# Long convolution and two MLPs: when the weights are decoded, how the last rows of z come back, when weights are loaded

## The chip, the cores and the metric

The kernel runs on one core of one Trainium2 chip. The metric is the device time of one execution in microseconds. Five engines work from queues of their own: PE (TensorE, the matmuls), DVE (VectorE), ACT (ScalarE), POOL (GpSimd) and SP (SyncE, which issues most DMAs). Each queue is taken in order: an instruction that waits for a semaphore holds up all that stand behind it on its engine.

## The reference, cut to what matters

```python
# x, v: (1, 12480, 128); pos_emb: (12480, 64)
h_filt = (np.maximum(pos_emb @ w1, 0.0) @ w2) * np.exp(-0.01 * pos)[:, None]
y = irfft(rfft(x * v, n=2*S) * rfft(h_filt, n=2*S))[:S]     # causal convolution, per channel
x = x * y
h = x @ moe_w_in;  g = np.where(h > 0, h, np.exp(np.minimum(h, 0)) - 1);  x = g @ moe_w_out
h = x @ moe2_w_in; g = np.maximum(h, 0) + alpha * np.minimum(h, 0);       out = g @ moe2_w_out
```

The sequence has 12480 rows of 128 channels, d_ff is 2048. The four MLP weights arrive as 64-bit words; the kernel decodes them into two float32 parts, a high one (rounded to the matmul's format) and a low one (what is left), and each MLP product is made of three matmuls: high x high, high x low, low x high.

## The kernel before, in words

**Stages.** The Fourier transform is split in two levels: 64 phases of 196 points, of which 99 frequencies f are kept. The first level (to about 108 us) leaves the transforms of `u` and `r` in SBUF (`ureg`, `sregs`). Then comes the *products loop*: 25 steps d (`ND`), each for four frequencies. Then the *inverse transform* `inv2` of tiles 0 and 1 and, from there to the end, the two MLPs over 26 tiles of up to 490 rows.

**One step d of the products loop.** The hooks of d run first (`run_hooks`). Then PE makes `b_h(d)` into the PSUM tile `prh`; ACT copies it to SBUF (line 338, called the `h` copy here); PE makes `z_mm(d - 3, (1,))`, `b_r(d + 1)` into the same `prh`, `b_u(d)` into one of two `pu` tiles and `z_mm(d - 2, (0,))`. `products(d)` multiplies on DVE (lines 353 and 377) and adds on POOL. `z_mm(d, (y,))` makes 16 matmuls into `pzz`; ACT copies them (line 394) into one of three staging buffers `zsts`, number (2d + y) % 3; SP writes the buffer to DRAM, `zlo` for y = 0, `zhi` for y = 1, 256 KB each (line 399). A staging buffer is free again when its write has landed.

**Decoding in the loop.** Sixteen pieces of 512 KB hold the weights; pieces 10 to 15 are decoded beside the loop (10 and 11 belong to wo1, 12 to 15 to wi1). `dec_load(j)` loads one, `dec_op(j, i)` is operation i of eleven. Operations 0 and 2 to 6 are DVE's and stand in `mid`, in the middle of `products`; operation 1 (`Abs`, line 108) and 7 (the cast to the high part, line 122) are ACT's and stand among the hooks, at the head of a step; 8 and 9 are POOL's, 10 writes wo1 back to DRAM. Operation 1 needs what 0 has read, 2 needs 1; 7 reads the array `b` that 4 made. For wo1 the cast's result lies in the array `e`, which operation 5 writes and 6 reads; for wi1 it goes to the weight's own place. With t the step of operation 0 (3, 6, 9, 12, 15, 18 for the pieces 10 to 15) the operations stand at

```
before: DVE 0 at t, 2 3 at t+1, 4 5 at t+2, 6 at t+3     ACT 1 at t+1, 7 at t+3
after:  DVE 0 at t, 2 3 at t+2, 4 at t+3, 5 6 at t+4     ACT 1 at t+2, 7 at t+5
```

**The way back.** `z_sb` holds z with the 99 frequencies on the partitions and 128 columns q of 128 values. `z_rows` reads rows of `zlo` into it, from step 18 on. The inverse transform of tiles 0 and 1 wants the columns 0 to 8 and 64 to 72 (`QA` = 9) of all 99 rows. For steps 23 and 24 these are not read from `zlo`: `z_mm` copies them from the staging buffer straight into `z_sb`, one small DMA for each row and column block, 14 in all (line 398), and then writes `zlo`. Behind the loop stand `z_mm` for steps 22 to 24, the second half of the products of steps 23 and 24 (`late`) and 4 + 8 matmuls whose result nothing reads (`idle_mm`, line 409; the profile counts two records for each).

**Weights.** The decoded wo1, wi2 and wo2 lie in DRAM. `reload` brings a high or a low part (1024 KB) back by a DMA that POOL issues (line 417). wo1's high part is loaded at step 14, its low part and wi2's high part at step 24, wi2's low part and both of wo2 in the MLPs. `inv2_load` (lines 446 to 455) loads `xT` and `finv` of a tile; for tiles 0 and 1 at step 23, `finv` being 303 and 379 KB.

**The order of the MLPs** is written out by hand: in slot s, chunk s of the first MLP begins, `o1_mm(s)` follows 5 slots later at first, and the second MLP starts in slot 23. `at(s, ...)` puts a load into slot s.

Of the kernel before, what the change touches and what calls it, by code (L numbers as in the profile page):

```python
# [19 lines left out]
P = 64  # L20
# [6 lines left out]
ND = 25  # L27
# [3 lines left out]
NFF = 16  # L31
# [8 lines left out]
def kernel(ctx: ExitStack, tc: tile.TileContext, posT, w1b, w2b, sc2, xva, xT,  # L40
                           fmat, fwin, gmat, wmat, finv, wi1, wo1, wi2, wo2, alphaT, out):
    nc = tc.nc
# [6 lines left out]
    zlo = dram.tile([NF, 128, D], F32, name="zlo")  # L49
    zhi = dram.tile([NF, 128, D], F32, name="zhi")  # L50
    wd = {nm: dram.tile([128, 2, 2048], F32, name=f"wd_{nm}") for nm in ("wi2", "wo2", "wo1")}
# [11 lines left out]
    def col(o, n):  # L63
        return ureg[:, o : o + n]

    z_sb = col(0, 128 * D)[:NF].rearrange("f (q c) -> f q c", c=D)
    MB = 128 * D
    wh = {}
# [4 lines left out]
    rreg = regp.tile([128, D * P], F32, name="rreg")  # L73
# [9 lines left out]
    parts = {}  # L83
# [47 lines left out]
    pieces = [(src, nm, k) for src, nm in ((wo2, "wo2"), (wi2, "wi2"), (wo1, "wo1"), (wi1, "wi1")) for k in range(4)]  # L131
# [148 lines left out]
    prh, pzz = (psp.tile([128, 1024], F32, name=x) for x in ("prh", "pzz"))  # L280
# [4 lines left out]
    def ysum(d):  # L285
        p, q = 512 * (d % 2), 1024 + 512 * (d % 3)
        v = rreg[:, p : p + 2 * (q - p)].rearrange("p (y r) -> p y r", y=2)[:, :, :512]
        return v.rearrange("p y (c e w) -> p y c e w", c=2, e=2)
# [7 lines left out]
    def rows(x):  # L296
        return slice(64 * x, 64 * x + 64)

    def b_r(d):
        for e in range(2):  # L300
            for r in range(2):
                for par in range(2):
                    f = fof(2 * d + e, par)
                    a = a_rs[0][:, f, r] if f < NR else a_rs[1][:, f - NR, r]
                    for half in range(2):
                        c = par ^ half
                        nc.tensor.matmul(prh[rows(c), 512 * half + 128 * e : 512 * half + 128 * e + 128], a[rows(half)],  # L307
                                         gts[d][rows(half), f - 4 * d, (64, 0)[r] : (192, 128)[r]], start=(r == 0), stop=(r == 1))
        for half in range(2):
            for par in range(2):  # L310
                nc.scalar.copy(rt[rows(half), 256 * par : 256 * par + 256], prh[rows(par ^ half), 512 * half : 512 * half + 256])
# [29 lines left out]
    nm = [0]  # L341
# [40 lines left out]
    def z_mm(d, ys):  # L382
        pz = prh if d == ND - 1 else pzz
        for i, y in enumerate(ys):
            for c in range(2):
                for cq in range(2):
                    for par in range(2):
                        nc.tensor.matmul(pz[rows(cq), 512 * par : 512 * par + 256], w_sb[rows(par), c, rows(cq)],
                                         ysum(d)[rows(par), y, c].rearrange("p e w -> p (e w)"),
                                         start=(y == 0 and c == 0), stop=(c == 1 and i == len(ys) - 1),  # L390
                                         skip_group_check=y == 1 and len(ys) == 1)
        n = min(4, NF - 4 * d)
        z = zsts[(2 * d + y) % 3]
        nc.scalar.copy(z.rearrange("q (e a) w -> q a e w", a=2), pz.rearrange("q (a h e w) -> q h a e w", a=2, h=2, e=2)[:, 0])
        if y == 0 and d >= ND - 2:
            for i in range(n):
                for q in (0, P):
                    nc.sync.dma_start(z_sb[4 * d + i : 4 * d + i + 1, q : q + QA], z[q : q + QA, i])
        nc.sync.dma_start((zlo, zhi)[y][4 * d : 4 * d + n].rearrange("f q c -> q f c"), z[:, :n])

    QA = 9

    def z_rows(f0, f1, q0, q1):
        nc.sync.dma_start(z_sb[f0:f1, q0:q1], zlo[f0:f1, q0:q1])

    def idle_mm(n, pz):
        for x in range(n):
            o = 512 * (x % 2)
            nc.tensor.matmul(pz[:, o : o + 512], w_sb[:, 0], rreg[:, 4096 : 4096 + 512], start=True, stop=True)
# [2 lines left out]
        for i, nm in enumerate(nms):  # L412
            wh.setdefault(nm[:3], {})[nm[3]] = t[:, 2048 * i : 2048 * i + 2048].rearrange("p (a b) -> p a b", b=128)

    def reload(nm, xs="hl"):
        for x in xs:
            nc.gpsimd.dma_start(wh[nm][x].rearrange("p a b -> p (a b)"), wd[nm][:, "lh".index(x), :])

    tiles = []
    for half in range(2):  # L420
        p0 = 0
# [5 lines left out]
    def width(t):  # L427
        half, p0, npz = tiles[t]
        return npz * (NI if half == 0 else NIH)

    def mwidth(t):
        return width(t) + width(t) % 2
# [10 lines left out]
        nout[0] += 1  # L443
        return spare[1 + nout[0] % 2]

    def inv2_load(t):
        half, p0, npz = tiles[t]
        ni = NI if half == 0 else NIH
        w, mw = width(t), mwidth(t)
        xt, fv = spare[t] if t < 2 else spare[0], fvs[t % 2]  # L450
        nc.sync.dma_start(xt[:, :w], xT[half][:, p0 * ni : p0 * ni + w])
        nc.sync.dma_start(fv[:, :npz], finv[half][:, p0 : p0 + npz])
        if mw > w:
            nc.gpsimd.memset(xt[:, w:mw], 0.0)
        pre[t] = (xt, fv)
# [23 lines left out]
    def when(d, fn, *args):  # L479
        hooks.setdefault(d, []).append((fn, args))  # L480
# [4 lines left out]
        when(0, dec_op, 9, i)  # L485
    for j, s, t in ((10, 2, 3), (11, 4, 6), (12, 6, 9), (13, 8, 12), (14, 12, 15), (15, 16, 18)):
        when(s, dec_load, j)
        for i, d in ((0, 0), (2, 1), (3, 1), (4, 2), (5, 2), (6, 3)):
            mid.setdefault(t + d, []).append((j, i))
        for i, d in ((1, 1), (7, 3), (8, 4), (9, 4), (10, 5))[: 5 if pieces[j][1] in wd else 4]:  # L490
            when(t + d, dec_op, j, i)
    for d, f0, f1, *qs in ((18, 0, 64, (64, 96)), (19, 0, 64, (96, 112), (32, 48)), (20, 0, 64, (16, 32), (48, 64)),
                           (21, 0, 64, (0, 16)), (22, 64, 80, (0, 64), (64, 112)), (24, 80, 88, (0, QA), (P, P + QA))):
        for q in qs:
            when(d, z_rows, f0, f1, *q)
    when(14, reload, "wo1", "h")
    for t in range(2):
        when(23, inv2_load, t)
    when(24, reload, "wo1", "l")
    when(24, reload, "wi2", "h")  # L500
    b_r(0)
    late = []
    for d in range(ND):
# [3 lines left out]
        h = b_h(d)  # L507
# [15 lines left out]
        if d == ND - 2:  # L523
            wb = spool_.tile([128, (NF - NR) * D], F32R, name="sb", bufs=1)
            take(wb, "wo1l", "wi2h")
    z_rows(88, 92, 0, QA)
    z_rows(88, 92, P, P + QA)
    z_mm(ND - 3, (1,))
    idle_mm(4, prh)
    z_mm(ND - 2, (0,))  # L530
    z_mm(ND - 1, (0,))
    for d, u, h in late:
        products(d, u, h, 1, 2)
    idle_mm(8, pzz)
    z_mm(ND - 2, (0, 1))
    inv2(0)
    inv2(1)
    z_mm(ND - 1, (1,))
    for f0, f1, *qs in ((80, 96, (QA, P), (P + QA, 128)), (96, 99, (QA, P), (P + QA, 128)), (0, 80, (112, 128))):
        for q in qs:  # L540
            z_rows(f0, f1, *q)
# [149 lines left out]
    def at(s, fn, *args):  # L691
        aux.setdefault(s, []).append((fn, args))
# [6 lines left out]
    for x in (0, 2, 1, 3):  # L699
        at((nlow - 2) * NFF + MID + 1, z_load, x)  # L700

    for s, nm, x in ((4, "wi2", "l"), (9, "wo2", "h"), (14, "wo2", "l")):
        at(s, reload, nm, x)
    TOT = NT * NFF
    o1_at, o2_at = {}, {}
# [131 lines left out]
```

## Time and profile before

| | |
|---|---|
| median of 3 runs | 1508.63 us (1504.62 to 1512.77) |
| the profiled execution: time / span | 1509.57 us / 1507.8 us |
| busy: PE / DVE / ACT / POOL | 94% / 84% / 72% / 63% |
| TensorE clock granted, mean | 0.976 |
| products loop begins / last step's `h` copy | 109 us / 311.87 us |
| first matmul of the inverse transform / of the MLPs | 346.17 us / 354.52 us |

A share of 1.00 for the clock is 2.4 GHz, a stretch wholly at the lower level of 1.2 GHz would show 0.50. A busy PE is not PE at its peak. In a line of a group or of the timeline, `out<-in` are the tiles written and read, `x16` is the number of instructions, and the square brackets hold the idle time of the engine before the instruction and what ended it. SPq is SP's queue: time in it is the issuing of DMAs, not their transfer. The DMA share is the mean busy share of the 16 DMA engines.

### The profile page before, as it was taken

To read this page: it belongs to the slowest core of one execution; us is meant where nothing else is said; L and a number is where in the kernel's file an instruction comes from. 1 tells how busy PE (TensorE), PEld (TensorE's weight loads), DVE (VectorE), ACT (ScalarE), POOL (GpSimd) and SP (SyncE) were. 2 spreads that over 40 slices of the span, in tenths; PEclk is the share of its full clock that TensorE was granted. 3 is DMA by queue.
4 is the path that set the end of the run, shared out by engine and by line. 5 is a ranking of instruction groups with operands and counts; after the bars stand their busy time and mean duration, and the time that the engine had idled before them with its cause. 6 is when DMAs were issued, how large, how long until landed. Compare 5 with 4: busy or idle time off the path is not lost.

```text
span 1507.8 us, 27199 instructions
## 1 busy us (share of the span) xinstructions
PE 1416.9 (94%) x10168; PEld 1196.7 (79%) x10168; DVE 1261.1 (84%) x1793; ACT 1081.4 (72%) x2041; POOL 944.8 (63%) x839
## 2 busy tenths in 40 slices
PE   6888677778999999999999999999999999999998
PEld 6876555647888888888888888888888888888897
DVE  5686556535999999999999999999999999999998
ACT  3454444424888888888888888888888888887884
POOL 3665455443666676666676666666666667666666
PEclk9999889889999999999999999999999999999999
DMA  8784445856200000000000500000000000000000
GB/s 255 228 264 140 140 128 159 196 153 113 78 23 25 8 18 25 24 25 24 8 18 25 192 29 24 15 17 18 24 25 24 24 8 18 25 24 21 7 8 13
DMA packets 57136, 97.61 MB, mean 65 GB/s; under 512 B 4642, under 2 KB 37604, under 8 KB 55306
## 3 DMA queue, kind: packets, MB, share of 16 engines
q1 hardware_dynamic: 53788, 84.79, 19.6%
q0 software_dynamic: 1296, 7.86, 1.5%
q10 hardware_dynamic: 1920, 3.21, 0.6%
q8 instruction: 80, 1.31, 0.4%
q14 instruction: 52, 0.43, 0.1%
HBM read 70.13 MB, written 25.66 MB: 64 GB/s over the span
## 4 chain that ended last, share of the span: by engine, by line
PE 84%; DMA 6%; DVE 5%; ACT 2%; issue 1%; SPq 1%; POOL 1%; POOLq 0%; DVEq 0%; ACTq 0%
PE psh L568 12%; PE pso L569 12%; PE pso L570 12%; PE psh L569 12%; PE pso L568 12%; PE psh L570 12%; PE pu L325 4%; PE psi L466 3%; PE prh L307 2%; DVE spreg L353 2%; ACT spreg L338 1%; DMA x<-in_xva_dram 1%; DMA ureg<-in_posT_dram 1%; PE pa L225 1%; DMA zhi<-rreg 1%
## 5 line engine op out<-in xcount | busy, mean ns | idle before, releaser
L591 POOL TENSOR_TENSOR g1l<-ureg,g1h 128x486 fp32r<-128x486 f32 (+3 forms) x313 | 364.7, 1165 | 202.5 <-ACT g1h L617 198.4
L591 POOL TENSOR_TENSOR g2l<-ureg,g2h 128x490 fp32r<-128x490 f32 (+3 forms) x315 | 346.2, 1099 | 122.3 <-ACT g2h L640 47.2
L629 DVE TENSOR_SCALAR ureg<-psh,al_sb 128x486 f32<-128x486 f32 (+3 forms) x416 | 296.0, 712 | 54.5 <-PE psh L570 53.9
L603 ACT ACTIVATE ureg<-psh 128x490 f32<-128x490 f32 (+2 forms) x393 | 225.6, 574 | 91.6 <-PE psh L570 88.0
L634 DVE SCALAR_TENSOR_TENSOR ureg<-psh,ureg 128x486 f32<-128x486 f32 (+3 forms) x416 | 274.1, 659 | 14.3
L611 DVE SCALAR_TENSOR_TENSOR ureg<-ureg,psh 128x486 f32<-128x486 f32 (+3 forms) x416 | 268.4, 645 | 4.0 <-ACT ureg L604 2.3
L617 ACT CAST g1h<-ureg 128x490 fp32r<-128x490 f32 (+3 forms) x405 | 240.0, 593 | 19.8 <-DVE ureg L611 18.0
L604 ACT ACTIVATE ureg<-ureg 128x490 f32<-128x490 f32 (+2 forms) x393 | 239.9, 610 | 12.5
L640 ACT CAST g2h<-ureg 128x490 fp32r<-128x490 f32 (+3 forms) x404 | 234.8, 581 | 8.5 <-DVE ureg L634 7.0
L568 PE MATMUL psh<-sb,sa 128*128 128x486 f32 (+3 forms) x416 | 160.8, 387 | 0.0
L568 PE MATMUL psh<-x2h,sb 128*128 128x486 f32 (+3 forms) x416 | 158.6, 381 | 1.1 <-ACT x2h L660 1.1
L569 PE MATMUL psh<-x2l,sb 128*128 128x486 f32 (+3 forms) x416 | 158.8, 382 | 0.4 <-DVE x2l L661 0.4
L569 PE MATMUL psh<-sb,sa 128*128 128x486 f32 (+3 forms) x416 | 158.8, 382 | 0.0
L570 PE MATMUL psh<-x2h,wc 128*128 128x486 f32 (+3 forms) x416 | 158.3, 381 | 0.0
L570 PE MATMUL psh<-sb,sa 128*128 128x486 f32 (+3 forms) x416 | 157.2, 378 | 0.0
L569 PE MATMUL pso<-g2l,wc 128*128 128x490 f32 (+3 forms) x404 | 155.5, 385 | 0.5 <-POOL g2l L591 0.5
L569 PE MATMUL pso<-g1l,sa 128*128 128x490 f32 (+3 forms) x405 | 155.5, 384 | 0.3 <-DVE g1l L591 0.2
L570 PE MATMUL pso<-g2h,wc 128*128 128x490 f32 (+3 forms) x404 | 154.9, 383 | 0.0
L568 PE MATMUL pso<-g1h,sa 128*128 128x490 f32 (+3 forms) x405 | 154.6, 382 | 0.0
L570 PE MATMUL pso<-g1h,sb 128*128 128x490 f32 (+3 forms) x405 | 154.4, 381 | 0.0
L568 PE MATMUL pso<-g2h,wc 128*128 128x490 f32 (+3 forms) x404 | 154.2, 382 | 0.0
L591 DVE TENSOR_TENSOR g1l<-ureg,g1h 128x490 fp32r<-128x490 f32 (+3 forms) x104 | 121.5, 1168 | 15.2 <-ACT g1h L617 4.0
(134 smaller groups left out, 2432.7 us busy)
## 6 DMA issues: line engine op xcount, KB each, us to landing
rreg<-in_gmat_dram SPq DMA_DIRECT2D x24, 384.0 KB
ureg<-in_finv_dram SPq DMA_DIRECT2D x24, 379.0 KB
ureg<-zhi SPq DMA_DIRECT2D x4, 1584.0 KB
x<-in_xva_dram SPq DMA_DIRECT2D x32, 196.0 KB
v<-in_xva_dram SPq DMA_DIRECT2D x32, 196.0 KB
zlo<-rreg SPq DMA_DIRECT2D x24, 256.0 KB
zhi<-rreg SPq DMA_DIRECT2D x24, 256.0 KB
ureg<-zlo SPq DMA_DIRECT2D x6, 512.0 KB
```

The lines of the kernel that those rows point to most:

```text
L325: nc.tensor.matmul(dst, gts[d][rows(half), f - 4 * d, g0 : g0 + 64], src, start=(x == 0), stop=(x == 2))
L568: nc.tensor.matmul(ps[:, :w], ah, bh[:, :w], start=start, stop=False)
L569: nc.tensor.matmul(ps[:, :w], ah, bl[:, :w], start=False, stop=False)
L570: nc.tensor.matmul(ps[:, :w], al, bh[:, :w], start=False, stop=stop)
L591: eng.tensor_tensor(lo[:, :w], e[:, :w], hi[:, :w], ALU.subtract)
L603: nc.scalar.activation(e[:, :w], ps[:, :w], AF.Relu, scale=-1.0)
L604: nc.scalar.activation(e[:, :w], e[:, :w], AF.Exp, scale=-1.0)
L611: nc.vector.scalar_tensor_tensor(e[:, :w], e[:, :w], -1.0, ps[:, :w], op0=ALU.add, op1=ALU.max)
L617: nc.scalar.copy(hi[:, :w], e[:, :w])
L629: nc.vector.tensor_scalar(e[:, :w], ps[:, :w], 0.0, al_sb[:, c : c + 1], op0=ALU.min, op1=ALU.mult)
L634: nc.vector.scalar_tensor_tensor(e[:, :w], ps[:, :w], 0.0, e[:, :w], op0=ALU.max, op1=ALU.add)
L640: nc.scalar.copy(hi[:, :w], e[:, :w])
```

## The change

Operations 1 and 7 of the decoding and those of DVE and POOL are put on other steps (the table above). The 14 small copies go; instead the staging buffers of steps 23 and 24 for y = 0 move to a part of `rreg` that is no longer used, and the columns 0 to 8 and 64 to 72 of rows 80 to 91 and 92 to 98 are read from `zlo` by two transfers (`z_first`), in place of the reads of rows 80 to 87 and 88 to 91 by two transfers each. The writes of y = 1 of steps 22 to 24 to `zhi` are held back until the inverse transform of tiles 0 and 1 and `z_mm(24, (1,))` are queued. `finv` of tiles 0 and 1 is loaded at step 21 in place of 23. At step 24 POOL loads 6 of 16 chunks of wo1's low part; the other 10 chunks (640 KB) come in slot 0 of the MLPs and wi2's high part in slot 2. Of the unread matmuls the first four go and eight become five.

```diff
...
                                          skip_group_check=y == 1 and len(ys) == 1)
         n = min(4, NF - 4 * d)
         z = zsts[(2 * d + y) % 3]
+        if y == 0 and d >= ND - 2:
+            o = 4864 + 768 * (d - ND + 2)
+            z = rreg[:, o : o + 512].rearrange("p (f w) -> p f w", f=4)
         nc.scalar.copy(z.rearrange("q (e a) w -> q a e w", a=2), pz.rearrange("q (a h e w) -> q h a e w", a=2, h=2, e=2)[:, 0])
-        if y == 0 and d >= ND - 2:
-            for i in range(n):
-                for q in (0, P):
-                    nc.sync.dma_start(z_sb[4 * d + i : 4 * d + i + 1, q : q + QA], z[q : q + QA, i])
-        nc.sync.dma_start((zlo, zhi)[y][4 * d : 4 * d + n].rearrange("f q c -> q f c"), z[:, :n])
+
+        def write():
+            nc.sync.dma_start((zlo, zhi)[y][4 * d : 4 * d + n].rearrange("f q c -> q f c"), z[:, :n])
+
+        if y == 1 and d >= ND - 3:
+            return write
+        write()
 
     QA = 9
 
     def z_rows(f0, f1, q0, q1):
         nc.sync.dma_start(z_sb[f0:f1, q0:q1], zlo[f0:f1, q0:q1])
+
+    def z_first(f0, f1):
+        dst, src = (t[f0:f1].rearrange("f (c q) w -> f c q w", c=2)[:, :, :QA] for t in (z_sb, zlo))
+        nc.sync.dma_start(dst, src)
 
     def idle_mm(n, pz):
         for x in range(n):
...
         for i, nm in enumerate(nms):
             wh.setdefault(nm[:3], {})[nm[3]] = t[:, 2048 * i : 2048 * i + 2048].rearrange("p (a b) -> p a b", b=128)
 
-    def reload(nm, xs="hl"):
-        for x in xs:
-            nc.gpsimd.dma_start(wh[nm][x].rearrange("p a b -> p (a b)"), wd[nm][:, "lh".index(x), :])
+    def reload(nm, x, c0=0, c1=NFF):
+        nc.gpsimd.dma_start(wh[nm][x][:, c0:c1].rearrange("p a b -> p (a b)"), wd[nm][:, "lh".index(x), 128 * c0 : 128 * c1])
 
     tiles = []
     for half in range(2):
...
         nout[0] += 1
         return spare[1 + nout[0] % 2]
 
-    def inv2_load(t):
+    def inv2_load(t, parts=(0, 1)):
         half, p0, npz = tiles[t]
         ni = NI if half == 0 else NIH
         w, mw = width(t), mwidth(t)
         xt, fv = spare[t] if t < 2 else spare[0], fvs[t % 2]
+        if 0 in parts:
+            nc.sync.dma_start(fv[:, :npz], finv[half][:, p0 : p0 + npz])
+        if 1 not in parts:
+            return
         nc.sync.dma_start(xt[:, :w], xT[half][:, p0 * ni : p0 * ni + w])
-        nc.sync.dma_start(fv[:, :npz], finv[half][:, p0 : p0 + npz])
         if mw > w:
             nc.gpsimd.memset(xt[:, w:mw], 0.0)
         pre[t] = (xt, fv)
...
         when(0, dec_op, 9, i)
     for j, s, t in ((10, 2, 3), (11, 4, 6), (12, 6, 9), (13, 8, 12), (14, 12, 15), (15, 16, 18)):
         when(s, dec_load, j)
-        for i, d in ((0, 0), (2, 1), (3, 1), (4, 2), (5, 2), (6, 3)):
+        for i, d in ((0, 0), (2, 2), (3, 2), (4, 3), (5, 4), (6, 4)):
             mid.setdefault(t + d, []).append((j, i))
-        for i, d in ((1, 1), (7, 3), (8, 4), (9, 4), (10, 5))[: 5 if pieces[j][1] in wd else 4]:
+        for i, d in ((1, 2), (7, 5), (8, 5), (9, 5), (10, 6))[: 5 if pieces[j][1] in wd else 4]:
             when(t + d, dec_op, j, i)
     for d, f0, f1, *qs in ((18, 0, 64, (64, 96)), (19, 0, 64, (96, 112), (32, 48)), (20, 0, 64, (16, 32), (48, 64)),
-                           (21, 0, 64, (0, 16)), (22, 64, 80, (0, 64), (64, 112)), (24, 80, 88, (0, QA), (P, P + QA))):
+                           (21, 0, 64, (0, 16)), (22, 64, 80, (0, 64), (64, 112))):
         for q in qs:
             when(d, z_rows, f0, f1, *q)
     when(14, reload, "wo1", "h")
     for t in range(2):
-        when(23, inv2_load, t)
-    when(24, reload, "wo1", "l")
-    when(24, reload, "wi2", "h")
+        when(21, inv2_load, t, (0,))
+        when(23, inv2_load, t, (1,))
+    when(24, reload, "wo1", "l", 0, 6)
     b_r(0)
     late = []
     for d in range(ND):
...
         if d == ND - 2:
             wb = spool_.tile([128, (NF - NR) * D], F32R, name="sb", bufs=1)
             take(wb, "wo1l", "wi2h")
-    z_rows(88, 92, 0, QA)
-    z_rows(88, 92, P, P + QA)
-    z_mm(ND - 3, (1,))
-    idle_mm(4, prh)
+    writes = [z_mm(ND - 3, (1,))]
     z_mm(ND - 2, (0,))
     z_mm(ND - 1, (0,))
+    z_first(80, 92)
+    z_first(92, 99)
     for d, u, h in late:
         products(d, u, h, 1, 2)
-    idle_mm(8, pzz)
-    z_mm(ND - 2, (0, 1))
+    idle_mm(5, pzz)
+    writes.append(z_mm(ND - 2, (0, 1)))
     inv2(0)
     inv2(1)
-    z_mm(ND - 1, (1,))
+    writes.append(z_mm(ND - 1, (1,)))
+    for write in writes:
+        write()
     for f0, f1, *qs in ((80, 96, (QA, P), (P + QA, 128)), (96, 99, (QA, P), (P + QA, 128)), (0, 80, (112, 128))):
         for q in qs:
             z_rows(f0, f1, *q)
...
     for x in (0, 2, 1, 3):
         at((nlow - 2) * NFF + MID + 1, z_load, x)
 
-    for s, nm, x in ((4, "wi2", "l"), (9, "wo2", "h"), (14, "wo2", "l")):
+    at(0, reload, "wo1", "l", 6, NFF)
+    for s, nm, x in ((2, "wi2", "h"), (4, "wi2", "l"), (9, "wo2", "h"), (14, "wo2", "l")):
         at(s, reload, nm, x)
     TOT = NT * NFF
     o1_at, o2_at = {}, {}
```

## Rows read from the trace of the kernel before

**Rows 1.** The page: PE's busy share in 40 slices of 37.7 us, in tenths.
```profile
PE   6888677778999999999999999999999999999998
```

**Rows 2.** Stages: length, busy us of PE, PEld, DVE, ACT, POOL; clock, DMA share, GB/s.
```profile
128.22:263.54 135.32, 98.87 (x2176) 77.85 (x2171) 79.01 (x108) 58.92 (x115) 68.63 (x56) 0.87 0.49 144
263.54:311.87 48.33, 37.14 (x848) 29.62 (x848) 26.43 (x35) 22.43 (x46) 27.63 (x24) 0.89 0.82 183
311.87:346.17 34.30, 23.62 (x184) 12.05 (x185) 7.65 (x12) 4.53 (x8) 7.75 (x11) 0.80 0.45 135
346.17:354.52 8.35, 7.48 (x88) 5.96 (x88) 1.80 (x3) 1.12 (x2) 0.14 (x1) 0.59 0.20 56
354.52:383.19 28.67, 26.94 (x132) 22.26 (x128) 26.04 (x49) 21.93 (x47) 17.53 (x19) 1.00 0.97 195
```

**Rows 3.** ACT's groups in the loop: busy, mean ns | idle before, releaser.
```profile
L108 ACT ACTIVATE ureg<-ureg 128x512 f32<-128x512 f32 x6 | 4.0, 663 | 19.2 <-DVE ureg L105 19.2
L122 ACT CAST sa<-ureg 128x512 fp32r<-128x512 f32 x4 | 2.5, 619 | 12.0 <-DVE ureg L116 12.0
L122 ACT CAST ureg<-ureg 128x512 fp32r<-128x512 f32 x2 | 1.2, 618 | 6.8 <-DVE ureg L118 6.8
```

**Rows 4.** Timeline, a disturbed step: start, us, engine, line, [idle before <- releaser].
```profile
219.25 0.66 ACT L108 ACTIVATE ureg<-ureg 128x512 f32<-128x512 f32 x1 [3.30 <-DVE ureg L105]
219.81 1.00 ACT L338 COPY spreg<-prh 128x1024 f32<-128x1024 f32 x1
220.86 1.85 PE L307 MATMUL prh<-rreg,sb 64*64 64x128 f32 x32 [3.77 <-ACT spreg L338]
```

**Rows 5.** Timeline, an undisturbed step.
```profile
298.19 1.01 ACT L338 COPY spreg<-prh 128x1024 f32<-128x1024 f32 x1 [0.29 <-PE prh L335]
299.25 1.10 PE L307 MATMUL prh<-rreg,sb 64*64 64x128 f32 x32 [0.20 <-ACT spreg L338]
300.17 1.92 PE L325 MATMUL pu<-ureg,rreg 64*64 64x256 f32 x48
303.66 1.09 PE L388 MATMUL pzz<-rreg,fw_sb 64*64 64x256 f32 x16
303.90 1.01 ACT L338 COPY spreg<-prh 128x1024 f32<-128x1024 f32 x1 [0.29 <-PE prh L335]
```

**Rows 6.** The chain of waits, loop and tail: start, us, what.
```profile
128.22 1.02 ACT spreg L338
263.54 1.01 ACT spreg L338
297.92 2.27 DMA zlo<-rreg
300.25 8.50 DMA ureg<-zlo
308.81 15.18 DMA zhi<-rreg
```

**Rows 7.** Timeline, the tail of the loop.
```profile
312.94 3.37 PE L325 MATMUL pu<-ureg,rreg 64*64 64x256 f32 x48
324.09 0.58 ACT L394 COPY rreg<-pzz 128x512 f32<-128x512 f32 x1 [10.28 <-DMA zhi<-rreg]
326.64 5.50 PE L409 MATMUL prh<-rreg,fw_sb 128*128 128x512 f32 x8
333.89 6.24 SPq L398 DMA_DIRECT2D ureg<-rreg  x8
346.17 0.39 PE L466 MATMUL pzz<-ureg 99*64 99x98 f32 x4 [3.19 <-DMA ureg<-rreg]
```

**Rows 8.** DMA issues in the loop, in the MLP's start: KB, us to landing.
```profile
sa<-wd_wo POOLq DMA_DIRECT2D x1, 1024.0 KB, 7.1
...
wc<-wd_wi POOLq DMA_DIRECT2D x1, 1024.0 KB, 16.6
```

**Rows 9.** Timeline of PE: the low part of wo1's seventh chunk.
```profile
366.61 0.34 PE L570 MATMUL pso<-g1h,sb 128*128 128x392 f32 x1
```

## The prediction

> **What bounds the kernel now.** I read the 40 slices of the page first, then the busy time by stage, then the stage that the change edits, line by line. In the slices [rows 1] PE is full from the eleventh slice on: from the start of the MLPs to the end TensorE is the bound, and nothing in the diff changes what is multiplied there. What can be won lies before. The stages [rows 2] are cut at the `h` copy (line 338) of steps 3, 18 and 24 of the products loop, at the first matmul of the inverse transform (346.17) and at the first matmul of the MLP (354.52). In the fifteen steps 3 to 18 no engine is full: PE 98.87 of 135.32 us at clock 0.87, DVE 79.01, transfers 0.49. So a chain of waits sets the pace, 135.32 / 15 = 9.02 us a step.
>
> The ACT groups of the loop [rows 3] name the wait. ACT sits idle 19.2 us ahead of six `Abs` (line 108) and 12.0 + 6.8 us ahead of six decoding casts (line 122), each time for DVE. One such step [rows 4]: the `Abs` waits 3.30 us for DVE's decoding operation of the step before, the `h` copy stands behind it in ACT's queue, and PE's next matmuls (line 307) wait 3.77 us for that copy. A step without such a wait [rows 5] runs from copy to copy in 303.90 - 298.19 = 5.71 us.
>
> **Part 1, ACT's decoding two steps behind DVE.** In steps 3 to 18 (128.22 to 263.54 [rows 6]) there are ten waits (pieces 10 to 14, `Abs` and cast). The excess over the undisturbed step is 15 x (9.02 - 5.71) = 49.7 us, so one wait costs 5.0 us: more than the idle time of 3 us, since PE drops to the lower clock behind it (its 32 matmuls of line 307 take 1.85 us there and 1.10 undisturbed [rows 4, 5]). After the change the `Abs` comes two steps behind the operation that it needs, and so does the cast of pieces 12 to 15. For pieces 10 and 11 (wo1) it does not: their cast writes over the array `e`, which DVE's operation 6 reads in the products of the step just before. So two of the ten waits stay, in steps 8 and 11: 10.0 us. Where two ACT operations (0.66 + 0.62 us [rows 3]) now come in one step, they push the `h` copy back by about 1.0 us, in steps 14 and 17, and a single one by 0.4 in step 5: 2.4 us. DVE's own work is reordered but equal, 79.01 / 15 = 5.27 us a step, still under 5.71. Transfers need 0.49 x 135.32 = 66 us. That fits into 100 us on the mean, and I add 2 us for moments in which a write is late for its staging buffer. Sum: 85.7 + 10.0 + 2.4 + 2 = 100.1 us, that is 35.2 less. Bounds: nothing gained (another wait takes over) to 49.7 - 10 = 39.7.
>
> In steps 18 to 24 the transfers are the next limit. They are busy 0.82 x 48.33 = 39.6 us there [rows 2], and the two `finv` loads now come at step 21, in front of them: 682 KB, at this stage's 183 GB/s 3.7 us. That is 43 us of transfers against about 6 x 5.71 + 1.6 = 36 us of compute. A read of the last z rows landed 8.50 us after its issue, and the write behind it left only when it was done [rows 6]; both stay. I take 42 us (the transfer sum, with a little of it still running when step 24 starts), 6 less; ends 36 and 48.3.
>
> **Part 2, the tail of the loop, 34.30 us** [rows 2]. In the trace, z of step 22 is copied only at 324.09, after 10.28 us of waiting for the `zhi` write that used the staging buffer before [rows 7]; that write took 15.18 us [rows 6], beside 2 MB of weights and the `finv` and `xT` loads. With 384 KB of weights there instead of 2 MB, and `finv` gone, I let the wait fall away. Then 14 small copies follow: SP issues the first 8 in 6.24 us [rows 7], 0.78 each, and the inverse transform starts at 346.17, behind the last of them.
>
> After the change, on the old time axis: the last `b_u` ends at 312.94 + 3.37 = 316.3. Four groups of z matmuls (1.09 us each [rows 5]), three ACT copies between and behind them (0.58 [rows 7]) and 0.6 of hand-over make 6.7: 323.0. The write to `zlo` takes 2.27 [rows 6] and its issue at most the 0.78 of a small copy, I take 0.4; the read back has its nearest row in that write, so the same 2.7: 328.4. This round trip through DRAM is a wait that the change adds; behind it on SP stand the three delayed `zhi` writes, the late z rows and the loads for tile 2, none of them needed before the third inverse transform, tens of us later. PE meanwhile runs five unread matmuls and z of step 23 again; with 5.50 us for four unread ones [rows 7], partly at the lower clock, 7 to 9 us from 322.4 on, with the z matmuls: 329.4 to 331.4. So the matmuls and the reading end about together; I take 330.3, 15.9 less. Ends: 8 less, if the copy still waits about 8 us for its buffer, and 19 less.
>
> The four unread matmuls in front of z(23) go outright; they stood on PE's path. The delayed `zhi` writes cost nothing as long as the second half of the output, far behind, reads them; they keep their three staging buffers until then, and no copy waits for these.
>
> From there to the MLP, 8.35 us at clock 0.59 [rows 2]. PE now comes to it from matmuls without a gap, so part of it runs at the higher level: 1.5 less, between 0 and 3.
>
> **Part 3, later weights.** From 354.52 on the transfers are busy 0.97 of 28.67 us [rows 2]. 640 KB of wo1 and 1024 KB of wi2 now come on top, and 256 KB of `zhi`. The seventh chunk of the low part of wo1 is needed at 366.61 [rows 9], 12.1 us after the start; its load can leave some 1 us after it. A 1024 KB load landed 7.1 us after its issue in the loop, but 16.6 us in this stage [rows 8]: nothing late by the one, 5.5 us late by the other. The loads of wi2 and wo2 queue behind it: 1.9 MB more at the 195 GB/s of this stage are 10 us, if nothing of it finds a gap. Either holds PE up where it would be full. I take +5, about the late landing or half of the 10, with the ends 0 and +12.
>
> The Trainium skill ("DMA: Bandwidth & Descriptors", section "Queues, rings and completion order") says that each DMA engine takes turns between the queues at packet granularity. By that rule the weights would move beside the slow z reads, and this term would be 0 and the time some 1451. The trace speaks against it here: the landing of 16.6 us against 7.1 in the loop [rows 8] looks like a load that stood behind others.
>
> **Sum**, against the profiled execution of 1509.57 (span 1507.8 and 1.8 around it; the median of the runs is 1508.63, 0.06% off, so I leave it): -35.2 - 6 - 15.9 - 1.5 + 5 = -53.6, so 1456 us.
>
> **Rivals.**
> - *Only the waits go, the clock stays low.* Of the idle time ahead of the six `Abs` and the four casts [rows 3] five and three lie in steps 3 to 18: 19.2 x 5/6 + 12.0 x 3/4 = 25.0, less 2.4, is 22.6 in place of 35.2: 1469. For it: clock 0.87 in all of this stage. Against: in the undisturbed step the 48 matmuls of `b_u` take 1.92 us [rows 5], and nothing is left that makes PE idle there.
> - *Transfers hide after all.* Steps 18 to 24 run at the pace of compute (-6) and the weights come in time (-5): 1445. For it: z reads are only wanted at the end. Against: the 8.50 and the 0.97.
> - *The weights are late*, by 12 and not 5, with PE idle in the first tile: 1463.
> - *Slower: the transfer queue is the bound everywhere.* The place is the SP queue with its three staging buffers: if each write lands late, ACT's copies wait for it in place of DVE, the loop keeps its 9 us a step, the tail keeps its 34 us, since the read back stands behind the same queue, and the loads put off now land late: wi2's second half stands behind 1.6 loads more, at 7.1 to 16.6 us each 11 to 27 us. That is 1521 to 1536, say 1527. It decides once the share of transfers in steps 3 to 18 comes near 1. Against: the 0.49.
>
> **How the numbers follow.** Forecast 42% (its own range 1447 to 1465), low clock 20%, hidden transfers 20%, late weights 13%, slower 5%. The range from 1437 to 1482 holds all but the last and a more extreme form of the others: the loop's gain lies between 24 and 40, the tail's between 8 and 19, the weights' cost between 0 and 12. A measurement of this kernel can tell about 0.5% (7.5 us) from no change. All cases but the last are faster by more than that: faster 0.95, within 0.01, slower 0.04.
>
> **What would show it.** Right: `h` copies 5.7 us apart in most of steps 4 to 18 with clock near 1; no ACT wait on DVE but in steps 8 and 11; no copy after step 24 waiting for a `zhi` write; the inverse transform some 18 us behind the last `h` copy and not 34; PE waiting for a weight load around the seventh chunk of wo1. Wrong: ACT copies waiting for `zlo` or `zhi` all along the loop, steps still over 8 us, or a transfer share near 1 from step 5 on.

## The result, and the profile after

The changed kernel takes 1466.47 us (median of 4 runs, 1463.73 to 1469.16) against 1506.62 for the kernel before: a ratio of 0.9727, 95% interval 0.9688 to 0.9766, 40 us less. The forecast was 1456, within 1437 to 1482. One of the four executions of the experiment e4 below took 1983.17 us at a mean granted clock of 0.648, far from its other three, and is left out of e4's times.

The page of the changed kernel, PE's row of the 40 slices (36.7 us each); the columns are those of [rows 1]:

```profile
PE   7888888769999999999999999999999999999998
```

In the loop's slices 4 to 7 PE shows 8, 8, 8, 8 where it showed 8, 6, 7, 7, and it is at 9 for good one slice earlier. The busy time by stage, cut at the same events as [rows 2] (the `h` copies of steps 3, 18 and 24, the first inverse-transform matmul, the first MLP matmul and the first matmul of the second MLP):

```profile
132.68:232.45 99.77, 86.45 (x2164) 68.05 (x2163) 76.88 (x101) 58.55 (x114) 64.28 (x53) 0.97 0.64 188
232.45:282.73 50.28, 37.26 (x864) 29.71 (x856) 32.00 (x42) 22.96 (x46) 32.15 (x27) 0.93 0.89 200
282.73:299.78 17.05, 14.55 (x170) 8.08 (x170) 7.66 (x12) 4.53 (x8) 7.61 (x10) 0.91 0.53 148
299.78:304.95 5.17, 4.44 (x89) 3.62 (x89) 1.80 (x3) 0.73 (x2) 0.00 (x0) 1.00 0.20 54
304.95:342.65 37.70, 27.27 (x131) 23.84 (x128) 25.74 (x49) 22.42 (x48) 18.81 (x21) 0.86 1.12 204
```

| stage, us | before | forecast | after |
|---|---|---|---|
| to the `h` copy of step 3 | 128.2 | 128.2 | 132.7 |
| steps 3 to 18 | 135.3 | 100.1 | 99.8 |
| steps 18 to 24 | 48.3 | 42.3 | 50.3 |
| to the inverse transform | 34.3 | 18.4 | 17.1 |
| to the MLP | 8.35 | 6.85 | 5.2 |
| MLPs, to the end of the span | 1153.3 | 1158.3 | 1162.4 |

The differences add up: +4.5 - 35.5 + 2.0 - 17.2 - 3.2 + 9.1 = -40.3, which is the difference of the two spans, 1507.8 and 1467.4, but for rounding.

ACT's groups in the loop (busy, mean ns | idle before, releaser): first the copies of z in the kernel before, then the changed kernel, whose other rows answer to [rows 3]:

```profile
L394 ACT COPY rreg<-pzz 128x512 f32<-128x512 f32 x42 | 24.7, 587 | 36.1 <-PE pzz L388 35.0 <-POOL rreg L379 1.1
```

```profile
L397 ACT COPY rreg<-pzz 128x512 f32<-128x512 f32 x43 | 25.3, 589 | 39.9 <-PE pzz L388 24.0 <-DMA zhi<-rreg 14.6 <-POOL rreg L379 1.1
...
L108 ACT ACTIVATE ureg<-ureg 128x512 f32<-128x512 f32 x6 | 4.1, 680 | 0.0
L122 ACT CAST sa<-ureg 128x512 fp32r<-128x512 f32 x4 | 2.5, 622 | 0.0
L122 ACT CAST ureg<-ureg 128x512 fp32r<-128x512 f32 x2 | 1.2, 617 | 6.8 <-DVE ureg L120 6.8
```

The reader is to see that 31.2 us of idle time ahead of `Abs` and four casts are gone to 0.0, that the two casts of wo1 (`ureg`) still wait 6.8 us for DVE, now for its operation 6 (L120), and that the copies of z have a new wait: 14.6 us for `zhi` writes, where the row of before has none (a single one, of 3.7 us, follows behind its window, which ends at 311 us). One step with such a cast, step 8, in the timeline of the changed kernel, beside [rows 4]:

```profile
163.84 0.69 DVE L120 SCALAR_TENSOR_TENSOR ureg<-ureg 128x512 f32<-128x512 uint32 x1
...
164.57 0.62 ACT L122 CAST ureg<-ureg 128x512 fp32r<-128x512 f32 x1 [3.42 <-DVE ureg L120]
165.09 0.66 ACT L108 ACTIVATE ureg<-ureg 128x512 f32<-128x512 f32 x1
...
165.65 0.99 ACT L338 COPY spreg<-prh 128x1024 f32<-128x1024 f32 x1
...
166.69 1.98 PE L307 MATMUL prh<-rreg,sa 64*64 64x128 f32 x32 [4.40 <-ACT spreg L338]
```

DVE's operation of step 7 ends, the cast follows at once, the `Abs` behind it has no wait of its own, and PE has waited 4.40 us for the `h` copy. Steps 8, 9, 11 and 12 come 9.93, 7.18, 9.93 and 7.37 us after the one before, most others 5.71.

The middle of steps 18 to 24 in the timeline of the changed kernel, copies of z and PE's gaps, and then SP's wait for z over all of these steps, before and after (us in total, times, longest):

```profile
245.57 0.59 ACT L397 COPY rreg<-pzz 128x512 f32<-128x512 f32 x1 [3.57 <-DMA zhi<-rreg]
...
253.76 0.59 ACT L397 COPY rreg<-pzz 128x512 f32<-128x512 f32 x1 [1.96 <-DMA zhi<-rreg]
...
260.61 0.32 PE L325 MATMUL pu<-ureg,rreg 64*64 64x128 f32 x1 [2.17 <-issue]
...
261.94 0.59 ACT L397 COPY rreg<-pzz 128x512 f32<-128x512 f32 x1 [3.59 <-DMA zhi<-rreg]
...
269.93 0.76 PE L325 MATMUL pu<-ureg,rreg 64*64 64x256 f32 x15 [2.54 <-issue]
```

```profile
SPq L404 <- DMA zlo<-rreg: 4.8, 2, 2.8
...
SPq L409 <- DMA zlo<-rreg: 12.0, 2, 8.5
```

ACT waits for `zhi` writes, PE twice over 2 us for nothing that the profile shows, and SP stands 12.0 us in front of z reads whose rows have not landed in `zlo`, with the next writes queued behind it. In the first tile of the MLPs, PE's wait and the landing of the load that it waits for (640.0 KB, us from issue to landing), which answers to [rows 8, 9]:

```profile
327.36 0.70 PE L582 MATMUL pso<-g1h,sb 128*128 128x392 f32 x1 [9.91 <-DMA sb<-wd_wo]
```

```profile
sb<-wd_wo POOLq DMA_DIRECT2D x1, 640.0 KB, 20.9
```

### The profile page after: what moved, and what is told of

The parts are those of the page before. It is cut to its first block, busy times and chain, and to the rows that moved or that the text cites. A ratio compares the mean times of both kernels' runs of the same rounds, so it can differ in the third digit from the quotient of the medians.

```text
span 1467.4 us, 27149 instructions
## 1 busy us (share of the span) xinstructions
PE 1395.7 (95%) x10154; PEld 1184.5 (81%) x10154; DVE 1269.8 (87%) x1793; ACT 1081.9 (74%) x2041; POOL 946.1 (64%) x840
## 4 chain that ended last, share of the span: by engine, by line
PE 88%; DMA 6%; DVE 2%; ACT 2%; issue 1%; POOL 0%; SPq 0%; POOLq 0%; ACTq 0%; DVEq 0%
PE psh L580 13%; PE pso L581 12%; PE pso L582 12%; PE psh L581 12%; PE pso L580 12%; PE psh L582 12%; PE pu L325 3%; PE psi L477 3%; PE pzz L388 2%; PE pa L225 2%; PE prh L307 2%; DMA sb<-wd_wo 1%; DMA ureg<-in_posT_dram 1%; ACT spreg L338 1%; PE prh L335 1%; DMA zhi<-rreg 1%
```

## The experiments

All kernels but e4 are the changed kernel with an edit; ratios are against the kernel before, run on the same chip. The stages are cut as above.

| kernel | us | ratio, 95% | 3 to 18 | 18 to 24 | to inverse | to MLP | MLPs |
|---|---|---|---|---|---|---|---|
| changed | 1466.5 | 0.9688 to 0.9766 | 99.8 | 50.3 | 17.1 | 5.2 | 1162.4 |
| e1 wo1 casts later | 1455.0 | 0.9614 to 0.9666 | 88.0 | 47.7 | 15.8 | 5.2 | 1164.0 |
| e2 wo1 low part whole | 1456.8 | 0.9632 to 0.9684 | 99.6 | 50.0 | 17.6 | 5.2 | 1153.5 |
| e3 z reads in the MLPs | 1449.2 | 0.9568 to 0.9647 | 101.5 | 38.9 | 15.2 | 6.8 | 1153.1 |
| e4 decoding alone | 1474.4 | 0.9715 to 0.9786 | 101.8 | 45.7 | 31.9 | 9.2 | 1153.3 |
| e5 all but decoding | 1501.6 | 0.9941 to 0.9971 | 135.3 | 49.1 | 17.3 | 5.2 | 1164.4 |
| e6 e1, e2 and e3 | 1436.0 | 0.9504 to 0.9533 | 89.0 | 38.8 | 15.2 | 5.2 | 1153.3 |
| e8 no unread matmuls | 1470.7 | 0.9737 to 0.9770 | 100.2 | 49.7 | 16.4 | 8.9 | 1156.8 |
| e9 small copies back | 1470.0 | 0.9730 to 0.9774 | 100.0 | 48.2 | 24.1 | 9.0 | 1157.3 |
| e10 late z reads put off | 1458.8 | 0.9645 to 0.9688 | 100.2 | 50.2 | 17.3 | 5.2 | 1153.3 |
| e11 rows 64 to 79 later | 1459.3 | 0.9650 to 0.9688 | 100.6 | 46.6 | 15.2 | 5.2 | 1160.3 |

The start of the loop (`h` copy of step 0) lies between 110.5 and 117.8 us in these profiles and at 111.1 and 116.9 in those of before and after, with the same program up to there. So single times carry some 7 us that belong to no edit, and the verdicts below go by stage. Stages differ from run to run as well. With the same program in them, steps 3 to 18 took 99.6 to 101.5 us (changed, e2, e3, e8 to e11), steps 18 to 24 took 48.2 to 50.3 (changed, e2, e8, e9, e10), and the way to the inverse transform, with the five unread matmuls and both reads, 15.2 to 17.6.

**e1: the wo1 casts one step later.**

```diff
-            when(t + d, dec_op, j, i)
+            when(t + d + (i >= 7 and pieces[j][1] in wd), dec_op, j, i)
```

> The changed kernel, with operations 7 to 10 of the two wo1 pieces one step later, so that their cast too comes two steps behind the operation it needs. Theory: the `h` copies of steps 8, 9, 11 and 12 come 9.93, 7.18, 9.93 and 7.37 us after the one before, because ACT's cast waits for DVE's operation 6; these four fall to 5.7 to 6.7 each, steps 3 to 18 from 99.8 to 88 to 90 us, and the kernel loses 10 to 11 us: 1455 to 1457 against 1466.5. Rival A: another wait (POOL's operations 8 and 9, or a write late for its staging buffer) takes the place, the four steps stay over 7.5 us. Rival B: steps 3 to 18 do get faster, but steps 18 to 24, where transfers are the limit, give it back (50.2 us become 55 to 60): 1463 to 1466.

ACT's groups in the loop up to 250 us, and the stages from step 3 to 18 and to 24:

```profile
L108 ACT ACTIVATE ureg<-ureg 128x512 f32<-128x512 f32 x6 | 4.1, 692 | 0.0
L122 ACT CAST sa<-ureg 128x512 fp32r<-128x512 f32 x3 | 1.9, 619 | 0.0
L122 ACT CAST ureg<-ureg 128x512 fp32r<-128x512 f32 x2 | 1.2, 620 | 0.0
```

```profile
128.60:216.62 88.02, 82.77 (x2164) 65.82 (x2163) 80.77 (x100) 58.04 (x114) 64.52 (x52) 1.00 0.72 214
216.62:264.30 47.68, 36.00 (x864) 28.56 (x856) 35.16 (x43) 22.99 (x45) 32.78 (x27) 0.96 0.94 214
```

No decoding operation of ACT waits any more, PE's clock is 1.00 through the stage, and steps 3 to 18 take 88.0 us, 11.8 less. Steps 18 to 24 don't give it back. The theory holds, rivals A and B fall.

**e4: the decoding alone, on the kernel before.**

```diff
-        for i, d in ((0, 0), (2, 1), (3, 1), (4, 2), (5, 2), (6, 3)):
+        for i, d in ((0, 0), (2, 2), (3, 2), (4, 3), (5, 4), (6, 4)):
-        for i, d in ((1, 1), (7, 3), (8, 4), (9, 4), (10, 5))[...]
+        for i, d in ((1, 2), (7, 5), (8, 5), (9, 5), (10, 6))[...]
```

> The kernel before with the new places of the decoding operations and nothing else of the change. Theory: steps 3 to 18 take 99 to 101 us (135.3 before), steps 18 to 24 some 48 to 52, the tail 34 and the MLPs 1153 as before: 33 to 37 us less, 1470 to 1474 against 1506.6. Rival A: the loop is faster but its transfers, now closer together, are given back in steps 18 to 24 and in the tail (over 90 us together, 82.6 before): 1478 to 1490. Rival B: the loop's gain comes from the other parts of the change: over 1495.

The stages from step 3 to 18, to 24 and to the inverse transform:

```profile
131.10:232.91 101.81, 88.16 (x2164) 69.45 (x2162) 76.91 (x101) 58.67 (x114) 64.23 (x53) 0.93 0.62 185
232.91:278.64 45.73, 35.09 (x864) 27.44 (x856) 32.04 (x42) 22.77 (x45) 31.31 (x26) 0.96 0.90 206
278.64:310.51 31.87, 22.70 (x184) 11.71 (x185) 7.65 (x12) 4.54 (x8) 8.97 (x12) 0.84 0.48 147
```

34.7 us less than the kernel before on this chip (1509.1), as expected: most of the gain of the change. Steps 3 to 18 take 101.8 us, just over the expected 99 to 101. The two stages behind take 45.7 + 31.9 = 77.6 us, not the 82.6 of before and less than the theory's 48 to 52 and 34, so rival A falls, and rival B with the time. The transfers of steps 18 to 24 add up to 0.90 x 45.73 = 41.2 us here and to 0.89 x 50.28 = 44.7 in the changed kernel, which loads `finv` two steps earlier. The 3.5 us between them are near the 3.7 that the prediction gave to these loads.

**e5: everything but the decoding** (the diff of e4, the other way round, on the changed kernel).

> The changed kernel with the decoding operations back in their old places. Theory: the parts add up. Steps 3 to 18 take 133 to 137 us as before, steps 18 to 24 45 to 50, from there to the inverse transform 16 to 18, to the MLP 5, and the MLPs 1160 to 1164, since the load put off to slot 0 still stands beside the slow z reads: 1493 to 1500 against 1507 to 1509 before. Rival: without the faster loop the transfers have room, the weights land in time, and the MLPs take 1153: 1484 to 1490.

The first tile's wait, in PE's timeline:

```profile
358.51 0.69 PE L582 MATMUL pso<-g1h,sb 128*128 128x392 f32 x1 [10.60 <-DMA sb<-wd_wo]
```

The tail gives 17 us and the way to the MLP 3; the weights put off to slot 0 take back 11. What is left is 7 us (1501.6 against 1508.7), 2 us short of the expected 1493 to 1500. The stages lie within theirs; the MLPs' 1164.4 is 0.4 over. The rival, that the weights come in time if the loop is slow, falls: the wait does not hang on the loop.

**e2: wo1's low part whole at step 24.**

```diff
-    when(24, reload, "wo1", "l", 0, 6)
+    when(24, reload, "wo1", "l")
-    at(0, reload, "wo1", "l", 6, NFF)
```

> The changed kernel, with all 16 chunks of wo1's low part loaded at step 24 and none in slot 0. Theory: PE's 9.91 us of waiting for chunk 7 in the first tile is that load standing beside the slow z reads; it goes, and the MLPs from their first matmul to the end take 1153 to 1155 us in place of 1162.5; 640 KB more at step 24 push the write and the read of the last z rows back by 0 to 2 us. So 7 to 10 us less: 1457 to 1460. Rival: the transfer queue as a whole is the limit there; PE then waits about as long for wi2 or wo2, and the MLPs still take over 1159 us: 1463 to 1467.

The load of wo1's low part among the DMA issues (KB each, us to landing):

```profile
sb<-wd_wo POOLq DMA_DIRECT2D x1, 1024.0 KB, 7.8
```

1024 KB land in 7.8 us at step 24, where the 640 KB needed 20.9 in slot 0. PE waits for no weight, the MLPs take 1153.5 us as before, and the way to the inverse transform is 0.5 us longer, within its spread. The theory holds: wi2 and wo2 behind it come in time, the queue as a whole is not the limit.

**e10: only the late z reads put off.** The five reads behind the loop fetch the columns of tile 2 alone; those of the other tiles come in the MLPs, one tile ahead, and the columns 112 to 127 of rows 0 to 79 in slot 80.

```diff
-    for f0, f1, *qs in ((80, 96, (QA, P), (P + QA, 128)), (96, 99, (QA, P), (P + QA, 128)), (0, 80, (112, 128))):
-        for q in qs:
-            z_rows(f0, f1, *q)
+    for f0, f1 in ((80, 96), (96, NF)):
+        z_first(f0, f1, QA, QA + PT)
...
+    for t in range(3, nlow):
+        for f0, f1 in ((80, 96), (96, NF)):
+            at((t - 2) * NFF + 4, z_first, f0, f1, tiles[t][1], tiles[t][1] + tiles[t][2])
+    at(5 * NFF, z_rows, 0, 80, 112, 128)
```

> The changed kernel with all z reads of the loop as they are; only the five late reads behind the loop go, and their columns beyond tile 2 are read in the MLPs, one tile ahead. Theory: it is these reads, into 16 partitions at about 4 us a packet, beside which wo1's 640 KB take 20.9 us. Without them PE does not wait for chunk 7 and the MLPs take 1153 to 1155 us, while steps 18 to 24 keep their 47 to 51: 1456 to 1459 against 1466.5. Rival: the backlog of the loop's z reads or the number of bytes delays the weights; the MLPs stay over 1159: 1463 to 1467.

The landing of the same load, issued in the same slot as in the changed kernel:

```profile
sb<-wd_wo POOLq DMA_DIRECT2D x1, 640.0 KB, 5.2
```

5.2 us in place of 20.9, no wait of PE for a weight, the MLPs back at 1153.3, and steps 18 to 24 unchanged. The backlog of the loop is as it was, so it is the late z reads that made wo1 late. Whether by their bytes or by their slow packets, e10 alone doesn't say; e11 has a sign.

**e3: the z reads of the loop put off as well.** `z_first` reads rows 0 to 63 at step 21 and 64 to 79 at step 22 for tiles 0 and 1; everything else comes behind the loop for tile 2 and in the MLPs for the others.

```diff
-    for d, f0, f1, *qs in ((18, 0, 64, (64, 96)), (19, 0, 64, (96, 112), (32, 48)), (20, 0, 64, (16, 32), (48, 64)),
-                           (21, 0, 64, (0, 16)), (22, 64, 80, (0, 64), (64, 112))):
-        for q in qs:
-            when(d, z_rows, f0, f1, *q)
+    when(21, z_first, 0, 64)
+    when(22, z_first, 64, 80)
```

> The changed kernel, but the loop and the stretch behind it read only the columns of z that the inverse transform of tiles 0 to 2 wants; the other columns are read in the MLPs, one tile ahead. Theory: in steps 18 to 24 ACT's copies wait for zhi writes that stand behind the z reads, and PE for its instructions, which come by the same DMA engines; without the reads these steps take 36 to 39 us in place of 50.2. Behind the loop 1.6 MB of slow reads go too, so the weights of slot 0 land in time or a few us late: 3 to 9 us more. Total 14 to 22 us less: 1445 to 1453. Rival A: something else sets the pace of steps 18 to 24 (decoding of piece 15, the low clock): over 46 us. Rival B: the reads cost the same in the MLPs, PE waits for them there: no less than 1460.

The stage from step 18 to 24, and the landing of wo1's 640 KB:

```profile
232.20:271.13 38.93, 34.89 (x868) 27.49 (x864) 34.49 (x42) 22.94 (x46) 31.04 (x26) 0.96 0.61 171
```

```profile
sb<-wd_wo POOLq DMA_DIRECT2D x1, 640.0 KB, 6.3
```

38.9 us in place of 50.3, with the transfers' share at 0.61 and not 0.89. The reads cost nothing in the MLPs, where PE is the bound: 1153.1. So without the z reads steps 18 to 24 are 11 us shorter. The reads are not the whole of it: e4 has them too, with `finv` at step 23, and takes 45.7. On the way to the MLP this kernel needs 6.8 us, at a granted clock of 0.75, in spite of its five unread matmuls.

**e11: rows 64 to 79 later.** Step 22 reads with `z_first(64, 80)` only; the other columns come behind the loop, in reads of rows 64 to 95.

```diff
-                           (21, 0, 64, (0, 16)), (22, 64, 80, (0, 64), (64, 112))):
+                           (21, 0, 64, (0, 16))):
+    when(22, z_first, 64, 80)
...
-    for f0, f1, *qs in ((80, 96, (QA, P), (P + QA, 128)), (96, 99, (QA, P), (P + QA, 128)), (0, 80, (112, 128))):
+    for f0, f1, *qs in ((64, 96, (QA, P), (P + QA, 128)), (96, 99, (QA, P), (P + QA, 128)), (0, 64, (112, 128))):
```

> The changed kernel in which step 22 reads only the columns of tiles 0 and 1 of the z rows 64 to 79; the other columns of these rows are read behind the loop, with those of rows 80 to 95. Theory: the two reads into 16 partitions (3.6 us a packet) hold up the zhi write behind them in the last steps only; steps 22 to 24 fall from 9.57 + 9.81 to 12 to 15 together and steps 18 to 24 to 43 to 46, while PE waits for wo1 as long as now or a little longer (MLPs 1161 to 1166): 1460 to 1466. Rival A: the reads of the 64 other rows in steps 18 to 21 are the cause as well for the last steps; 18 to 24 stay over 47. Rival B: the whole gain of the smaller z reads lies here, steps 18 to 24 under 41.

46.6 us, just outside the theory's 43 to 46 and short of rival A's 47; steps 23 and 24 come after 11.25 and 5.72 us, 17.0 together where 12 to 15 were expected. Against the 48.2 to 50.3 of the kernels with the same loop, the two reads of step 22 cost some 2 to 4 us; the rest, down to e3's 38.9, goes with the larger reads of steps 18 to 21. How it divides within a step stays open. The time, 1459.3, is just under the expected 1460.

The late reads are larger here, 2437 KB in place of 1685, but rows 64 to 95 go into 32 partitions where rows 80 to 95 went into 16, and the 640 KB of wo1 land in 17.7 us in place of 20.9; PE waits 6.8 us for them in place of 9.91. In the trace the packets of 28 KB of these reads take 2.2 us on the mean, and 3.6 in the changed kernel. This speaks for the slow packets and against the number of bytes, though no run varies the partitions alone.

**e8: no unread matmuls** (`idle_mm(5, pzz)` taken out).

> The changed kernel without its five unread matmuls. In the changed kernel they end at 297.1, z of step 23 follows (1.96 us) and ACT's copy of it, and the inverse transform starts at 299.8. Theory: they stand on PE's path by some 1 to 2 us, since the last read of z lands at about the same time; without them PE idles until that landing, the inverse transform starts 15.5 to 17 us after the last h copy (17.1), and the stretch from there to the MLP gets longer by 0 to 3 us at the lower clock: 1464 to 1468, no difference that can be told. Rival A: they are pure cost, 3 to 4.5 us less in all. Rival B: they are what keeps the clock up, 3 us or more longer in all.

PE's timeline at the start of the inverse transform and at chunk 7, and the stretch from there to the MLP:

```profile
294.00 2.88 PE L477 MATMUL pzz<-ureg 99*64 99x98 f32 x32 [4.45 <-DMA ureg<-zlo]
...
319.41 0.44 PE L581 MATMUL pso<-g1h,sb 128*128 128x392 f32 x1 [4.05 <-DMA sb<-wd_wo]
```

```profile
293.90:302.90 9.00, 8.19 (x89) 6.70 (x89) 1.80 (x3) 1.12 (x2) 0.35 (x1) 0.51 0.06 16
```

PE idles 4.45 us for the last z read, the inverse transform starts 16.4 us after the last `h` copy (17.1 with them), and then runs at clock 0.51: 8.9 us to the MLP and not 5.2. Behind that it waits 4.05 us for wo1 and not 9.91, since the load's landing, not PE's start, sets that moment. The time, 1470.7, has an interval that overlaps the changed kernel's. So the five matmuls buy 3.7 us of clock; the 0.7 us of delay is less than the spread of that stage. The first part is rival B's, but no difference in time can be told. They are no guarantee: e3 has them and ran that stretch at 0.75.

**e9: the small copies again**, in place of the second read.

```diff
+        if y == 0 and d >= ND - 2:
+            for i in range(n):
+                for q in (0, P):
+                    nc.sync.dma_start(z_sb[4 * d + i : 4 * d + i + 1, q : q + QA], z[q : q + QA, i])
...
-    z_first(92, 99)
```

> The changed kernel with the 14 small copies of the last z rows again, in place of the second read from zlo. Theory: SP needs 0.77 us for each, 10.8 in all behind the copy of z of step 23 (about 290.5 in the changed kernel) with one zlo write between, and the last lands at 303 to 304, so the inverse transform starts 20 to 22 us after the last h copy and not 17.1: 3 to 5 us longer, 1469 to 1472. Rival: PE's unread matmuls and z of step 23 hide them, under 1 us.

The chain of waits: the first of the fourteen, the `zlo` write behind them, the inverse transform (start, us, what):

```profile
286.81 0.76 SPq L402
...
297.38 0.46 SPq L405
...
301.62 2.90 PE pzz L482 x32
```

24.1 us to the inverse transform, 7.0 more and beyond the 20 to 22 expected, and 9.0 to the MLP, at a granted clock of 0.50 in this stretch. The read of rows 80 to 91 stands behind the copies on SP (issued at 297.89), so its landing is part of the 7 us. In the MLPs 5.1 of these 10.8 come back: wo1 lands in 8.4 us and PE does not wait for it. It waits for a cast of ACT, which waits for a `zhi` write (us in total, times, longest):

```profile
ACT g1h L633 <- DMA zhi<-rreg: 4.7, 1, 4.7
...
PE pso L584 <- ACT g1h L633: 3.7, 1, 3.7
```

The second transfer in place of the copies is worth 7 us by stage. By the medians it is 3.5 us, and the intervals overlap: no difference in time can be told.

**e6: e1, e2 and e3 together.**

> The three edits together on the changed kernel: the casts of the two wo1 pieces one step later, wo1's low part whole at step 24, and the columns of z beyond tiles 0 to 2 read in the MLPs. Theory: each removes a wait of its own, so the stages take 88 to 90 (steps 3 to 18), 37 to 40 (18 to 24), 15 to 17, 5 to 7 and 1153 to 1155 us: 1430 to 1437. Rival: the freed transfers were one resource, and what the z reads give is what the weights' load gave too; PE or the staging buffers wait elsewhere: 1440 to 1450, with a stage over these bounds.

The stages, cut as before:

```profile
131.97:220.97 89.00, 83.05 (x2164) 65.36 (x2162) 80.70 (x100) 58.16 (x115) 64.50 (x52) 1.00 0.70 211
220.97:259.81 38.84, 34.62 (x868) 27.20 (x864) 35.05 (x43) 23.07 (x45) 31.93 (x26) 0.96 0.60 170
259.81:275.04 15.23, 12.89 (x171) 7.19 (x163) 7.65 (x12) 4.48 (x7) 9.15 (x12) 1.00 0.64 183
275.04:280.21 5.17, 4.45 (x89) 3.63 (x89) 1.79 (x3) 0.73 (x2) 0.00 (x0) 1.00 0.18 51
280.21:308.20 27.99, 26.45 (x130) 22.09 (x126) 25.31 (x47) 21.31 (x46) 17.92 (x20) 1.00 0.84 231
```

1436.0 us, ratio 0.9504 to 0.9533: 30 us faster than the changed kernel. The three stages that the edits aim at are each within 1 us of what the edit had given alone, so the three waits were separate.

## Why the prediction was right, and where a term was not

The time lies within the wide range, and 1.5 us outside the forecast's own 1447 to 1465. Its number is nearest to those of two rivals, 1463 for late weights and 1469 for a low clock. The spans show where the profiled kernel misses: 4.5 us before step 3, 8.0 in steps 18 to 24 and 4.1 in the MLPs on one side, 0.3, 1.3 and 1.7 in the other stages on the other.

**Steps 3 to 18: right in mechanism; the size owes something to luck.** 35.2 us were forecast and 35.5 came. Ten waits at 5.0 us each, of which two stay for the wo1 casts' write over `e`, is what the trace and e1 show: 11.8 us for the two, where the prediction had 10.0. The 2 us that it added for late writes did not come, no copy in these steps waits for one, and the two misses cancel. The rival "the clock stays low" falls with the stage's 0.97. e4, with this edit alone, gains 33.5 us there.

**Steps 18 to 24: the step of the prediction that failed.** "I take 42 us (the transfer sum...)" measured 50.3. The sum was about right, 0.89 x 50.28 = 44.7 us of transfers against 43; wrong was to let the stage last only as long as its transfers. They don't run without gaps: SP waits 12.0 us for rows of z to land before it may issue their reads, and the copies wait 14.6 us for the writes behind these reads, while PE has another 4.7 us of gaps. In the loop of before the first two were 4.8 and 3.7 us. So 2.0 us were lost where 6 were to be won. How the 8 us divide among these waits is not shown: in e4 the copies wait 14.2 us, PE has no such gaps, and the stage takes 45.7. The rival "transfers hide after all" (36 us) is what e3 comes near to, 38.9, only by taking the reads away.

**The tail: right.** 15.9 forecast, 17.2 measured; the copy of step 22 does not wait for a `zhi` write, and the round trip through DRAM takes 5.4 us (e8's chain of waits has 2.10 for the write and 3.28 for the read), as priced. To the MLP 3.2 us in place of 1.5, just beyond the upper end of 3 that was given: the clock was at 1.00. That nothing needs the delayed `zhi` writes for tens of us is not so. By the code the MLPs' buffers take the place of `rreg`, and their first cast waits for such a write:

```profile
308.19 0.52 ACT L629 CAST g1h<-ureg 128x392 fp32r<-128x392 f32 x1 [0.98 <-DMA zhi<-rreg]
```

That is 1 us here, for which PE does not wait; in e9, where the writes are later, PE loses 3.7 us by it.

**Weights: right mechanism, term too small.** 5 forecast, 9.1 measured. PE waited 9.91 us for the load that was named; it took 20.9 us to land, beyond the 16.6 of [rows 8], beside the late z reads, as e10 shows. That wi2 and wo2 would add to it, as half of the reason given, did not happen: in e2 and e10 PE waits for no weight. By the rule of the Trainium skill ("DMA: Bandwidth & Descriptors", "Queues, rings and completion order") that queues take turns, the prediction would have set the term to 0. The trace agrees with the turns, since the load's packets (309.7 to 326.1 us) lie among the 28 KB packets of the z reads (307.4 to 326.1); it does not bear out the 0, with 640 KB in 20.9 us beside the z reads and 5.2 us without them.

**Outside the steps.** 4.5 us came from the part before step 3, which the change does not touch; e3, with the same program there, had 130.7 and e8 127.7 in place of 132.7. Its cause was not looked for.

## What to carry to other kernels

An operation that an in-order engine runs for a side job should wait only for work that is a whole step old; check it operand by operand, because a buffer that is written over can tie it to the step just before although its input is long ready. A sum of transfer times is a lower bound for a stage, not an estimate: look for the points at which the issuing queue waits for data that must land first. Before a load is put off to a later stage, look at what the transfer queue holds at that moment; here 9 us of the 20 won in the tail went back that way.

## What was not expected of the hardware

The late z reads hold up a load of another queue: 640 KB from POOL's queue took 20.9 us beside 1.7 MB of z reads, and 5.2 us when most of these were put off (e10), while the share of the DMA engines was 1.12 at only 204 GB/s. In e11 a larger amount, most of it into 32 partitions where it was 16, held up the load less (17.7 us).

With the z reads in the loop, PE had gaps of 2.17 and 2.54 us for which the profile names no wait; in e3, without the reads, gaps of this kind came to 0.3 us in steps 18 to 24. The profile counts seven packets of 16 KB on a queue that it calls `instruction` in these steps:

```profile
q8 instruction: 7, 0.11, 1.1%
```

Two of them, at 257.87 us (for 1.32 us) and at 267.28 (for 1.26), land 1.4 us before PE starts again behind the two gaps. Between 60 and 300 us the traces of the twelve kernels hold 22 gaps of PE of over 0.9 us without a named wait, and each ends 1.2 to 1.7 us after such a packet has landed. This points to PE waiting for its instructions. That the z reads make them late is not shown: e4, with the reads and a share of 0.90, has seven such packets in these steps and no such gap, and e6, without the reads, has one gap of 1.0 us in steps 3 to 18.

Without the five matmuls that nobody reads, PE idles 4.45 us and the next 9 us run at a granted clock of 0.51 (e8); with them in that place the stretch ran at 1.00 in the changed kernel and at 0.75 in e3.
